# Three passes instead of two ahead of the memory rows' turn, later output passes, and a second work area for the left probabilities

## The chip, the core and the metric

The kernel runs on one core of a Trainium2 chip. The metric is the device time of one execution in microseconds (us). Before the change the median of three runs is 1904.54 us (1896.93 to 1905.54). Engines are named as in the profile: PE is the matrix engine (PEld its weight loads), DVE the vector engine, ACT the scalar engine, POOL and SP the two that issue most transfers. A transfer is a DMA.

## What is computed

The input is one sequence of 2048 rows of 1024 numbers, cut into 64 segments of 32 rows. Each segment is put behind 8 memory rows, goes through attention with 32 heads of 128, and its first 8 output rows are the memory of the next segment, so the segments form a chain.

```python
xn = layernorm(x)
for s in range(64):
    h = concat(mem, xn[32 * s:32 * s + 32])
    q, k, v = h @ Wq, h @ Wk, h @ Wv
    o = softmax(mask(q @ k.T * scale)) @ v @ Wo
    mem, out[s] = o[:8], o[8:]
return x + concat(out) + moe(xn)
```

The second summand, `moe`, picks two rows by a router score and sends them through a gated layer; it runs after the last segment.

## The kernel before

**Weights.** The three projections and the output projection are cut into 64 granules of 128 x 2048 (512 KB each). Granules 0 to 47 are six phases of eight (Wq, Wk for heads 0 to 15 and 16 to 31, then Wv), 48 to 63 are the output projection, two heads each. 44 granules are resident in on-chip memory. The 20 listed in `STREAMED` are loaded again for every segment, through five slots of a pool (`wstream`, tile `g`); two of them (6 whole, three quarters of 25) are kept in the PSUM memory and copied back, so 19 loads per segment are left. SP issues them in the order of use; a load waits until its slot has been read for the last time.

**Main rows and left rows.** A segment has 40 rows with the memory. 32 of them (8 memory rows and the first 24 rows of the segment) depend on the segment before and go through the phases as "main" rows (line L771, PSUM tile `PSm`, weights `ST`; output projection L571 into `WO`, weights `OT`). The last 8 rows of each segment, the "left" rows, depend on no memory for their q, k and v, so they are handled for four segments at once: a group `G` is four segments, `j` is the place of a segment in its group. For a group there are seven units of left passes: `q0`, `q1`, `k0`, `k1`, `v0`, `v1` with eight passes each (L564, tile `PSl`, weights `STL`), and `o`, the output projection, with 16 (L571 with tile `WL`, weights `OTL`). One pass is one granule times the left rows. All units share one PSUM tile (tag `accl`), so they run one after another.

**The order.** It is written out by hand. `PASSES` gives for each unit the places `(j, phase, kc)` and the granules whose passes run there; `kc` is the place in a phase of eight, phase 6 is the output projection (16 places), and 7 and 8 stand for the two places at the end of a segment. `COPIES` says where a finished unit is copied out of PSUM and on which engine. `hooks` do the same for attention work. Every engine runs its own queue in the order of this program.

**The end of a segment.** After the last output pass DVE adds the result to `X` (L840), PE turns the memory rows (L293, `mem_to_st`), DVE copies them into the next `ST` (L312), and the next segment's phase 0 begins. `run_passes(7, 0)` stands ahead of the turn, `run_passes(8, 0)` behind it:

```python
        nc.vector.tensor_tensor(out=OB[:, :], in0=WO[:, 0:256], in1=OB[:, :], op=ALU.add)
        ...
        run_passes(7, 0)
        if s + 1 < NSEG:
            mem_to_st(OB, nxt["st"])
        run_passes(8, 0)
```

**Attention of a segment.** `scores(half)`, `exponent()` (ACT, L663), `soften(half)` (DVE, L668 to L679) and `attend(half, ph)` (PE L693 and L695, then copies L702 into `OT` and L704 into `OTL`). `soften` writes the left probabilities into a zeroed work area, 8 blocks of 32 columns, and turns that with one 128x256 transpose (L679). For `j` of 1 to 3 the work area is the part of `OTL` that belongs to segment 3 of the group; at `j == 3` `attend(0, 0)` and `attend(0, 1)`, which stand behind `soften(1)` in the program, write the left outputs of heads 0 to 15 over the first half of it. At `j == 0` the work area is another tile, `BX`.

**The output rows of the left rows.** For unit `o` the sum with `x` is formed in tile `OL` (DVE, L593) and stored with four transfers of 16 KB by POOL (L596). `OL` has the tag `stl`, one buffer that it shares with `STL`, the turned left rows of the next group. `STL` is written by ACT (L307) in phase 6 at `w == 12` of the segment with `j == 0`, and the first user is the pass of unit `q0` at place (0, 7, 0). So at `j == 0` the four stores of `OL` must have landed before L307 may write.

Of the kernel before, what the change touches and what calls it, by code (L numbers as in the profile page):

```python
# [8 lines left out]
BF16 = mybir.dt.bfloat16  # L9
F32 = mybir.dt.float32  # L10
U32 = mybir.dt.uint32
ALU = mybir.AluOpType
# [17 lines left out]

UNIT_PHASE = {"q0": 0, "k0": 1, "q1": 2, "k1": 3, "v0": 4, "v1": 5, "o": 6}
PASSES = {
# [11 lines left out]
}  # L44

COPIES = {"q0": (1, 1, 0, "scalar"), "q1": (1, 5, 7, "vector"), "k0": (2, 2, 0, "scalar"), "k1": (3, 1, 0, "scalar"),
          "v0": (3, 4, 7, "scalar"), "v1": (3, 5, 7, "scalar"), "o": (0, 4, 3, "vector")}


@with_exitstack  # L50
def kernel(
# [16 lines left out]
    nc = tc.nc  # L68
    P = 128
# [3 lines left out]
    SEG = int(A_seg_len)  # L73
# [10 lines left out]
    XL = M  # L84
    NK = M + SEG
# [32 lines left out]
    one = ctx.enter_context(tc.tile_pool(name="one", bufs=1, reuse_waits="tile"))  # L118
# [78 lines left out]
    for s in range(4):  # L197
        nc.vector.tensor_copy(out=SELM[:, s, :, 0:XM],
                              in_=IDENT[:, 32 * s:32 * s + XM].unsqueeze(1).to_broadcast([P, 4, XM]))
        nc.vector.tensor_copy(out=SELL[:, s, :, :],  # L200
                              in_=IDENT.rearrange("p (s c) -> p s c", c=32)[:, :, XM:SEG])
# [304 lines left out]
    def left_out():  # L506
        if "otl" not in group:
            group["otl"] = one.tile([P, H, 4, XL], BF16, tag="otl", name="OTL")
        return group["otl"]
# [94 lines left out]
    for s in range(NSEG):  # L604
        G, j = divmod(s, 4)
# [6 lines left out]
        QT, KT, PTs, OT, nxt, sums = {}, {}, {}, {}, {}, {}  # L612
# [52 lines left out]
        def soften(half):  # L665
            S8 = SPS.rearrange("p i a k -> p (i a) k")
            DN = one.tile([P, 8], F32, tag="nm", name="DN")
            nc.vector.tensor_reduce(out=DN[:, :], in_=S8, axis=AX.X, op=ALU.add)  # L668
            nc.vector.reciprocal(out=DN[:, :], in_=DN[:, :])
            PT2 = one.tile([P, 2, 4, 64], BF16, tag=("bA", "bE")[half], name="PT2")  # L670
            PTm, PTl = PT2[:, 0], PT2[:, 1]
            PM = PTl.rearrange("p i q -> p (i q)").rearrange("p (b k) -> p b k", b=8)
            PLt = zeros_and_left()
            dnb = DN[:, :].unsqueeze(2)
            nc.vector.tensor_tensor(out=PM, in0=S8[:, :, 0:32], in1=dnb.to_broadcast([P, 8, 32]), op=ALU.mult)
            nc.vector.tensor_tensor(out=PLt[:, :, j, :], in0=S8[:, :, 32:NK],
                                    in1=dnb.to_broadcast([P, 8, XL]), op=ALU.mult)
            nc.vector.transpose(out=PTm.rearrange("p i q -> p (i q)"), in_=PM.rearrange("p b k -> p (b k)"))
            nc.vector.transpose(out=PTl.rearrange("p i q -> p (i q)"), in_=PLt.rearrange("p b s r -> p (b s) r"))  # L679
            PTs[half] = (PTm, PTl)  # L680

        def attend(half, ph, turn_too=None):
            if half not in OT:
                OT[half] = one.tile([P, 4, 4, SEG], BF16, tag=("kt", "bC")[half], name="OT")
                if half == 0:
                    nxt["wo"] = psA.tile([P, 512], F32, tag="acc", name="WO")
                sums[half] = [BS[:, 0:4 * NK] if half else nxt["wo"][:, 256:256 + 4 * NK], OPB]
            PTm, PTl = PTs[half]
            for il in range(4):
                for jl in range(2):  # L690
                    q0 = 32 * (2 * ph + jl)
                    o = sums[half][jl][:, il * NK:(il + 1) * NK]
                    nc.tensor.matmul(o, lhsT=VM[half][q0:q0 + 32, il * P:(il + 1) * P], rhs=PTm[q0:q0 + 32, il, 0:NK],  # L693
                                     start=True, stop=False, tile_position=(q0, 0), skip_group_check=True)
                    nc.tensor.matmul(o, lhsT=VL[half][q0:q0 + 32, il * P:(il + 1) * P], rhs=PTl[q0:q0 + 32, il, 0:NK],  # L695
                                     start=False, stop=True, tile_position=(q0, 0), skip_group_check=True)
            if turn_too is not None:
                turn_too()
            for jl in range(2):
                ov = sums[half][jl].rearrange("p (i q) -> p i q", i=4)  # L700
                copy = nc.scalar.copy if half == 0 or jl == 0 else nc.vector.tensor_copy
                copy(out=OT[half][:, 2 * ph + jl, :, :], in_=ov[:, :, 0:SEG])  # L702
                h0 = 16 * half + 8 * ph + 4 * jl
                copy(out=left_out()[:, h0:h0 + 4, j, :], in_=ov[:, :, SEG:NK])  # L704
# [3 lines left out]
        def zeros_and_left():  # L708

            z = left_out()[:, :, 3, :] if j or s == 0 else nxt["bx"][:, 0:256].rearrange("p (h r) -> p h r", r=XL)  # L710
            return z.rearrange("p (b s) r -> p b s r", s=4)
# [37 lines left out]
        hook(2, 6, lambda: scores(0))  # L749
        hook(3, 4, exponent)  # L750
        hook(3, 4, lambda: soften(0))
        if s + 1 < NSEG:
            hook(2, 4, lambda: load_seg(s + 1))
# [3 lines left out]
        hook(4, 6, lambda: scores(1))  # L757
        hook(5, 0, exponent)
        hook(5, 0, lambda: soften(1))
        hook(5, 4, lambda: attend(0, 0))  # L760
        hook(5, 6, lambda: attend(0, 1))

        for p, (mat, half) in enumerate(PHASES):
# [54 lines left out]
        for w in range(16):  # L818
            if w == 5:
                attend(1, 0)  # L820
            if w == 8 and s + 1 < NSEG:
                attend(1, 1, lambda: turned.append(turn(xn, BS[:, 160:288].bitcast(BF16))))
                nxt["st"] = new_st(turned[0])
            elif w == 8:
                attend(1, 1)
            if w == 12 and left_too is not None:
                STL = new_stl(turn(left_too))
            Gv = granule(48 + w)
            project(WO, w, Gv, lhs_main, w == 15, first=(w == 0))
            held[48 + w] = Gv  # L830
            run_passes(6, w)
            if w == 9 and s + 1 < NSEG:
                new_lx(s + 1)
                bring_back(1, nc.scalar.copy)
                bring_back(2, nc.vector.tensor_copy)
            if w == 11 and j == 3:
                xl_of[0] = load_left(G, one.tile([P, 256], BF16, tag="stl", name="OL")[:, :])
            release(6, w)
# [129 lines left out]
```

## Time and profile before

| what | value |
|---|---|
| median of 3 runs | 1904.54 us |
| the profiled execution, its own time | 1902.86 us |
| its span in the trace | 1901.0 us |
| granted TensorE clock, mean | 0.953 |
| PE busy | 1588.8 us (84%) |
| DVE busy | 895.1 us (47%) |
| ACT busy | 685.6 us (36%) |
| POOL busy | 441.7 us (23%) |
| bytes moved by DMA | 704.02 MB, mean 370 GB/s |
| the segments' adds (L840), first and last | 128.4 and 1843.0 us |

The span is the time from the first to the last instruction in the trace; the rest of the execution's own time lies around it. Busy matmul time is modelled and pipelined: four matmuls of 128x512 that belong to one pass follow each other at a few ns, and one row of the profile says 0.39 us for them, while passes follow each other every 0.21 us or so. A segment is the stretch between two rows of L840; in the middle of the run these lie some 27 us apart.

### The profile page before, as it was taken

To read this page: it belongs to the slowest core of one execution; us is meant where nothing else is said; L and a number is where in the kernel's file an instruction comes from. 1 tells how busy PE (TensorE), PEld (TensorE's weight loads), DVE (VectorE), ACT (ScalarE), POOL (GpSimd) and SP (SyncE) were. 2 spreads that over 40 slices of the span, in tenths; PEclk is the share of its full clock that TensorE was granted. 3 is DMA by queue.
4 is the path that set the end of the run, shared out by engine and by line. 5 is a ranking of instruction groups with operands and counts; after the bars stand their busy time and mean duration, and the time that the engine had idled before them with its cause. 6 is when DMAs were issued, how large, how long until landed. Compare 5 with 4: busy or idle time off the path is not lost.

```text
span 1901.0 us, 82443 instructions
## 1 busy us (share of the span) xinstructions
PE 1588.8 (84%) x36008; PEld 883.5 (46%) x36008; DVE 895.1 (47%) x2922; ACT 685.6 (36%) x1923; POOL 441.7 (23%) x882
## 2 busy tenths in 40 slices
PE   3658888888888898898888988988888888988864
PEld 1224545454454544445454544445454444545443
DVE  5824544455445544544455444544544454445430
ACT  1213333333343433343333333334333343433320
POOL 3211213222131222213121322213132221312220
PEclk8569999999999999999999999999999999999985
DMA  9999999999999999999999999999999999999998
GB/s 365 410 355 392 358 373 370 386 371 366 379 370 383 356 369 358 381 381 356 388 352 376 367 374 366 371 374 368 382 336 383 367 353 380 369 385 359 363 386 334
DMA packets 232089, 704.02 MB, mean 370 GB/s; under 512 B 39296, under 2 KB 61232, under 8 KB 231728
## 3 DMA queue, kind: packets, MB, share of 16 engines
q1 hardware_dynamic: 194384, 662.92, 91.9%
q0 software_dynamic: 28704, 27.96, 4.6%
q10 hardware_dynamic: 8640, 7.87, 1.2%
q8 instruction: 282, 4.62, 0.9%
q14 instruction: 79, 0.65, 0.1%
HBM read 685.93 MB, written 22.16 MB: 372 GB/s over the span
## 4 chain that ended last, share of the span: by engine, by line
DMA 54%; PE 37%; DVE 4%; issue 2%; ACT 1%; SPq 1%; ACTq 0%; DVEq 0%
DMA g<-wsc 45%; PE PSm L771 19%; PE WO L571 6%; PE PSl L564 3%; PE BT L621 3%; PE WL L571 2%; DMA XP<-in_A_x_dram 2%; DMA MW<-in_B_w_gate_dram 1%; DMA MW<-in_B_w_up_dram 1%; DMA g<-in_A_Wv_dram 1%; DMA g<-in_A_Wq_dram 1%; DMA wres<-in_A_Wv_dram 1%; DMA g<-in_A_Wk_dram 1%; DMA wres<-in_A_Wo_dram 1%; PE BS L644 1%
## 5 line engine op out<-in xcount | busy, mean ns | idle before, releaser
L771 PE MATMUL PSm<-wres,ST 128*32 128x512 bf16 x8448 | 710.6, 384 | 17.0 <-issue 8.6
L771 PEld LDWEIGHTS <-ST 128*32 128x32 bf16 x12288 | 329.1, 96 | 401.5 <-issue 186.8
L771 PE MATMUL PSm<-g,ST 128*32 128x512 bf16 x3588 | 363.4, 388 | 97.3 <-DMA g<-wsc 71.4
L571 PEld LDWEIGHTS <-OT 128*32 128x32 bf16 x8192 | 219.1, 98 | 152.0 <-issue 132.2
L790 ACT CAST XB<-PSm 128x512 bf16<-128x512 f32 x256 | 149.8, 585 | 312.8 <-PE PSm L771 308.1
L571 PE MATMUL WO<-wres,OT 128*32 128x256 bf16 x5632 | 242.7, 282 | 15.4 <-issue 8.4
L480 POOL DMA_DIRECT2D LX<-ql_d x63 | 33.6, 533 | 832.1 <-ACT OT L702 402.9
L571 PE MATMUL WO<-g,OT 128*32 128x256 bf16 x2560 | 134.3, 284 | 77.5 <-DMA g<-wsc 68.2
L564 PE MATMUL PSl<-wres,STL 128*32 128x512 bf16 x2112 | 191.9, 389 | 0.2 <-ACT VL L805 0.2
L842 POOL DMA_DIRECT2D out_dram<-X x256 | 129.5, 513 | 213.6 <-DVE X L840 165.5
L273 POOL DMA_DIRECT2D X<-in_A_x_dram x256 | 129.6, 511 | 187.1 <-PE PSm L771 88.1
L377 DVE COPY g<-BT 128x512 bf16<-128x512 bf16 x63 | 26.7, 425 | 307.2 <-ACT QT L629 256.5
L373 ACT COPY BK<-KEPT 128x512 bf16<-128x512 bf16 x126 | 75.8, 602 | 121.7 <-PE WO L571 121.7
L629 ACT COPY QT<-BT 128x512 bf16<-128x512 bf16 x128 | 74.9, 585 | 113.8 <-PE BT L621 113.1
L840 DVE TENSOR_TENSOR X<-WO,X 128x256 bf16<-128x256 f32 x64 | 27.2, 425 | 179.1 <-PE WO L571 179.1
L564 PEld LDWEIGHTS <-STL 128*32 128x32 bf16 x3072 | 83.9, 98 | 56.1 <-issue 9.8
L621 PEld LDWEIGHTS <-XB 128*128 128x128 bf16 x1024 | 58.9, 98 | 108.1 <-ACT XB L790 63.2
L693 PEld LDWEIGHTS <-VM 32*128 32x128 bf16 x2048 | 67.6, 91 | 85.1 <-issue 72.0
L800 ACT CAST VM<-PSm 128x512 bf16<-128x512 f32 x128 | 75.9, 593 | 78.1 <-PE PSm L771 76.7
L621 PE MATMUL BT<-IDENT,XB 128*128 128x128 bf16 x1024 | 102.6, 223 | 1.4 <-ACT QKL L499 1.4
L653 DVE TENSOR_TENSOR BS<-BS,CT 128x96 f32<-128x96 f32 (+1 forms) x256 | 59.6, 233 | 84.7 <-PE BS L646 80.2
L702 ACT CAST OT<-BS 128x128 bf16<-128x128 f32 x128 | 34.0, 265 | 181.3 <-PE BT L695 87.9
(170 smaller groups left out, 2428.2 us busy)
## 6 DMA issues: line engine op xcount, KB each, us to landing
g<-wsc SPq DMA_DIRECT2D x1134, 512.0 KB, 6.0
LX<-ql_d POOLq DMA_DIRECT2D x63, 128.0 KB, 5.9
g<-wsc SPq DMA_DIRECT2D x63, 128.0 KB, 5.2
ql_d<-XBl ACTq DMA_DIRECT2D x60, 128.0 KB, 5.4
MW<-in_B_w_gate_dram SPq DMA_DIRECT2D x16, 448.0 KB, 9.0
MW<-in_B_w_up_dram SPq DMA_DIRECT2D x16, 448.0 KB, 9.1
wres<-in_A_Wk_dram SPq DMA_DIRECT2D x12, 512.0 KB, 12.3
MW<-in_B_w_down_dram SPq DMA_DIRECT2D x12, 512.0 KB, 10.4
```

Of the source, the lines that this page charges most:

```text
L273: nc.gpsimd.dma_start(out=X[s % 2][32 * g:32 * g + XM, :], in_=x2[s * SEG:s * SEG + XM, 256 * g:256 * (g + 1)])
L373: copy(out=back[c][:, :], in_=KEPT_COLS[KEPT_WHOLE][c])
L564: nc.tensor.matmul(PSl[32 * jq:32 * jq + 32, :], lhsT=STL[:, g % KC, :], rhs=part(Gv, jq), start=first_, stop=last_, tile_position=(0, 32 ...
L571: nc.tensor.matmul(PS[32 * g:32 * g + 32, 0:256], lhsT=lhs(h), rhs=Gv[:, D * hs + 256 * g:D * hs + 256 * (g + 1)], start=(first and hs == ...
L621: nc.tensor.transpose(out=PTq[:, il, :, :].rearrange("p j r -> p (j r)"), in_=XB[:, il * P:(il + 1) * P], identity=IDENT[:, :])
L629: nc.scalar.copy(out=QT[half][:, :, :], in_=pv)
L653: nc.vector.tensor_tensor(out=S4, in0=S4, in1=m, op=ALU.add)
L693: nc.tensor.matmul(o, lhsT=VM[half][q0:q0 + 32, il * P:(il + 1) * P], rhs=PTm[q0:q0 + 32, il, 0:NK], start=True, stop=False, tile_position ...
L771: nc.tensor.matmul(PSm[32 * jq:32 * jq + 32, :], lhsT=ST[:, kc, :], rhs=part(Gv, jq), start=(kc == 0), stop=(kc == KC - 1), tile_position= ...
L790: nc.scalar.copy(out=XB[:, :], in_=PSm[:, :])
L800: nc.scalar.copy(out=VM[half][:, :], in_=PSm[:, :])
L842: nc.gpsimd.dma_start(out=out2[s * SEG:s * SEG + XM, 256 * g:256 * (g + 1)], in_=OB[32 * g:32 * g + XM, :])
```

## The change

Three edits, in one table and in two functions.

1. Units `q0`, `k0`, `k1` and `o` get three passes at place (j, 7, 0) and two at (j, 8, 0), where they had two and two. The fifth pass is taken from a place inside the phases: granule 7 from (1, 0, 7), 14 from (2, 1, 6), 24 from (2, 4, 1), 54 from (0, 0, 3). All the moved granules are resident.
2. The other output passes of the group before, at `j == 0`, start at (0, 2, 4) instead of (0, 0, 3) and end at (0, 5, 1) instead of (0, 4, 2); the sum and the stores of `OL` move from (0, 4, 3) to (0, 5, 3).
3. In `soften(1)` at `j == 3`, the work area is split. Blocks 0 to 3 are the new tile `Z`, 128 columns behind the 512 of `OT[0]` in the same buffer, zeroed by DVE; blocks 4 to 7 stay where they were. One product and one transpose become two of half the width. `attend` no longer makes `OT[0]` where `soften` has.

```diff
-    "q0": {(0, 7, 0): [0, 1], (0, 8, 0): [3, 4], (1, 0, 2): [2], (1, 0, 5): [5], (1, 0, 6): [6], (1, 0, 7): [7]},
+    "q0": {(0, 7, 0): [0, 1, 3], (0, 8, 0): [4, 7], (1, 0, 2): [2], (1, 0, 5): [5], (1, 0, 6): [6]},
...
-    "k0": {(1, 7, 0): [8, 10], (1, 8, 0): [11, 12], (2, 1, 1): [9], (2, 1, 5): [13], (2, 1, 6): [14], (2, 1, 7): [15]},
-    "k1": {(2, 3, 1): [25], (2, 3, 5): [29], (2, 4, 1): [24], (2, 4, 5): [26], (2, 7, 0): [27, 28], (2, 8, 0): [30, 31]},
+    "k0": {(1, 7, 0): [8, 10, 11], (1, 8, 0): [12, 14], (2, 1, 1): [9], (2, 1, 5): [13], (2, 1, 7): [15]},
+    "k1": {(2, 3, 1): [25], (2, 3, 5): [29], (2, 4, 5): [26], (2, 7, 0): [24, 27, 28], (2, 8, 0): [30, 31]},
...
-    "o": {(3, 6, 3): [50], (3, 6, 5): [53], (3, 6, 8): [56], (3, 6, 11): [59], (3, 6, 14): [62], (3, 7, 0): [48, 49],
-          (3, 8, 0): [51, 52], (0, 0, 3): [54], (0, 1, 1): [55], (0, 2, 0): [57], (0, 2, 4): [58], (0, 3, 0): [60],
-          (0, 3, 4): [61], (0, 4, 2): [63]},
+    "o": {(3, 6, 3): [50], (3, 6, 5): [53], (3, 6, 8): [56], (3, 6, 11): [59], (3, 6, 14): [62], (3, 7, 0): [48, 49, 51],
+          (3, 8, 0): [52, 54], (0, 2, 4): [55], (0, 3, 0): [57], (0, 3, 4): [58], (0, 4, 2): [60], (0, 4, 6): [61],
+          (0, 5, 1): [63]},
...
-          "v0": (3, 4, 7, "scalar"), "v1": (3, 5, 7, "scalar"), "o": (0, 4, 3, "vector")}
+          "v0": (3, 4, 7, "scalar"), "v1": (3, 5, 7, "scalar"), "o": (0, 5, 3, "vector")}
...
-            nc.vector.tensor_tensor(out=PLt[:, :, j, :], in0=S8[:, :, 32:NK],
-                                    in1=dnb.to_broadcast([P, 8, XL]), op=ALU.mult)
+            apart = half == 1 and j == 3
+            if apart:
+                OT[0] = one.tile([P, 640], BF16, tag="kt", name="OT")
+                Z = OT[0][:, 512:640]
+                nc.vector.memset(Z, 0.0)
+                parts = [(slice(0, 4), Z.rearrange("p (b s r) -> p b s r", b=4, s=4)), (slice(4, 8), PLt[:, 4:8])]
+                OT[0] = OT[0][:, 0:512].rearrange("p (i j r) -> p i j r", i=4, j=4)
+            else:
+                parts = [(slice(0, 8), PLt)]
+            for bs, z in parts:
+                n = bs.stop - bs.start
+                nc.vector.tensor_tensor(out=z[:, :, j, :], in0=S8[:, bs, 32:NK],
+                                        in1=dnb[:, bs].to_broadcast([P, n, XL]), op=ALU.mult)
             nc.vector.transpose(out=PTm.rearrange("p i q -> p (i q)"), in_=PM.rearrange("p b k -> p (b k)"))
-            nc.vector.transpose(out=PTl.rearrange("p i q -> p (i q)"), in_=PLt.rearrange("p b s r -> p (b s) r"))
+            for bs, z in parts:
+                nc.vector.transpose(out=PTl.rearrange("p i q -> p (i q)")[:, 32 * bs.start:32 * bs.stop],
+                                    in_=z.rearrange("p b s r -> p (b s) r"))
```

What it moves on the engines stands in the order of the program's instructions; a row names the line, the operation, and what is written from what, and where asked for, the semaphores that it waits for (`DVE_49` counts DVE's finished work, and so on).

On ACT, the copies behind `attend(0, 0)` in a segment with `j == 3`, before:

```order
L704 CAST OTL<-WO 128x4x8 [waits DVE_49,Pool_49]
L702 CAST OT<-BT 128x128 [waits PE_49]
L704 CAST OTL<-BT 128x4x8
L702 CAST OT<-WO 128x128 [waits PE_49]
L704 CAST OTL<-WO 128x4x8
```

and with the change (`attend` has moved down by 14 lines):

```order
L718 CAST OTL<-WO 128x4x8 [waits Pool_49]
L716 CAST OT<-BT 128x128 [waits PE_49]
L718 CAST OTL<-BT 128x4x8
L716 CAST OT<-WO 128x128 [waits PE_49]
L718 CAST OTL<-WO 128x4x8
```

The first copy into `OTL` no longer waits for DVE; its place and that of the others in ACT's queue are the same.

On PE, the matmuls at the end of a segment with `j == 0` (one row of each pass; `wres0` is resident granule 0, and so on), before:

```order
L571 MATMUL WO_24085<-wres63_1247,OT_24195 32x256
L564 MATMUL PSl_24351<-wres0_210,STL_24310 32x512
L564 MATMUL PSl_24351<-wres1_212,STL_24310 32x512
L293 MATMUL BT_134<-IDENT_125,X0_130 128x128
L564 MATMUL PSl_24351<-wres3_218,STL_24310 32x512
L564 MATMUL PSl_24351<-wres4_222,STL_24310 32x512
L771 MATMUL PSm_24371<-wres0_210,ST_24264 32x512
```

and with the change:

```order
L571 MATMUL WO_24109<-wres63_1247,OT_24219 32x256
L564 MATMUL PSl_24375<-wres0_210,STL_24334 32x512
L564 MATMUL PSl_24375<-wres1_212,STL_24334 32x512
L564 MATMUL PSl_24375<-wres3_218,STL_24334 32x512
L293 MATMUL BT_134<-IDENT_125,X0_130 128x128
L564 MATMUL PSl_24375<-wres4_222,STL_24334 32x512
L564 MATMUL PSl_24375<-wres7_228,STL_24334 32x512
L785 MATMUL PSm_24399<-wres0_210,ST_24288 32x512
```

One more pass stands ahead of the turn (L293), and granule 7's pass has come forward out of phase 0. The passes ahead of the turn read `STL`.

On DVE, the sum of the left output rows in a segment with `j == 0`, before (L679 ends `soften(0)`, the second L653 begins `scores(1)`):

```order
L679 STREAM_TRANSPOSE PT_23928<-BX 128x256 [waits DVE_49]
L593 TENSOR_TENSOR OL<-WL,OL 128x256 [waits PE_49]
L653 TENSOR_TENSOR BS<-BS,CT 128x4x24 [waits PE_49]
L655 TENSOR_SCALAR BS<-BS,CT 128x4x8 [waits DVE_49]
L653 TENSOR_TENSOR BS<-BS,CT 128x4x8 [waits DVE_49]
```

and with the change (L691 now ends `soften(1)`):

```order
L689 STREAM_TRANSPOSE PT_24068<-PT_24068 128x256 [waits DVE_49]
L691 STREAM_TRANSPOSE PT_24068<-BX 128x256 [waits DVE_49]
L593 TENSOR_TENSOR OL<-WL,OL 128x256 [waits PE_49]
L267 COPY RI<-BS 128x1
L268 RECIPROCAL RI<-BS 128x1
```

The sum has moved from between the two softmaxes of the segment to behind the second one, past the eleven rows from L653 to L679; POOL's four stores and, in ACT's queue, `STL` (L307) follow it as before.

More of the change, by code (lines that the diff above doesn't have):

```diff
@@ L675, in soften @@
             nc.vector.tensor_tensor(out=PM, in0=S8[:, :, 0:32], in1=dnb.to_broadcast([P, 8, 32]), op=ALU.mult)
-            nc.vector.tensor_tensor(out=PLt[:, :, j, :], in0=S8[:, :, 32:NK],
-                                    in1=dnb.to_broadcast([P, 8, XL]), op=ALU.mult)
+            apart = half == 1 and j == 3
[11 more added lines that the diff above has]
+                                        in1=dnb[:, bs].to_broadcast([P, n, XL]), op=ALU.mult)
             nc.vector.transpose(out=PTm.rearrange("p i q -> p (i q)"), in_=PM.rearrange("p b k -> p (b k)"))
-            nc.vector.transpose(out=PTl.rearrange("p i q -> p (i q)"), in_=PLt.rearrange("p b s r -> p (b s) r"))
+            for bs, z in parts:
+                nc.vector.transpose(out=PTl.rearrange("p i q -> p (i q)")[:, 32 * bs.start:32 * bs.stop],
+                                    in_=z.rearrange("p b s r -> p (b s) r"))
             PTs[half] = (PTm, PTl)
         def attend(half, ph, turn_too=None):
-            if half not in OT:
-                OT[half] = one.tile([P, 4, 4, SEG], BF16, tag=("kt", "bC")[half], name="OT")
+            if half not in sums:
+                if half not in OT:
+                    OT[half] = one.tile([P, 4, 4, SEG], BF16, tag=("kt", "bC")[half], name="OT")
                 if half == 0:
```

## The prediction

> **What bounds the kernel now.** I read the page's shares first, then the busy share of the transfers by stretches, then who waits for whom, then the timeline of one group of segments.
>
> ```profile
> PE 1588.8 (84%) x36008; PEld 883.5 (46%) x36008; DVE 895.1 (47%) x2922; ACT 685.6 (36%) x1923; POOL 441.7 (23%) x882
> q1 hardware_dynamic: 194384, 662.92, 91.9%
> DMA packets 232089, 704.02 MB, mean 370 GB/s; under 512 B 39296, under 2 KB 61232, under 8 KB 231728
> DMA 54%; PE 37%; DVE 4%; issue 2%; ACT 1%; SPq 1%; ACTq 0%; DVEq 0%
> ```
>
> The chain of waits changes between transfers (54%) and PE (37%): the streamed granules are the bound, and PE where it frees the slots late. q1 alone, SP's queue, takes 91.9% of the engines' time. So a microsecond of PE is worth something only where the transfers stand idle because of it. The stretches show where that is; the columns end with granted clock, DMA share and GB/s.
>
> ```profile
> 950.00:955.00 5.00, 5.00 (x120) 2.52 (x120) 3.53 (x11) 2.19 (x5) 0.00 (x0) 1.00 1.02 373
> 960.00:965.00 5.00, 4.14 (x138) 3.01 (x132) 2.31 (x10) 2.46 (x11) 0.00 (x0) 1.00 0.96 361
> 965.00:970.00 5.00, 3.06 (x107) 2.60 (x107) 0.72 (x3) 1.07 (x4) 2.88 (x5) 1.00 0.87 298
> 970.00:975.00 5.00, 4.49 (x101) 2.44 (x91) 0.95 (x3) 1.17 (x2) 3.52 (x7) 1.00 1.03 351
> 975.00:980.00 5.00, 4.33 (x78) 2.28 (x82) 1.74 (x7) 1.96 (x4) 3.20 (x6) 1.00 0.86 305
> 980.00:985.00 5.00, 5.00 (x128) 2.88 (x128) 4.04 (x14) 2.31 (x6) 0.00 (x0) 1.00 0.97 313
> 985.00:990.00 5.00, 4.36 (x122) 2.21 (x114) 3.76 (x12) 2.74 (x13) 2.40 (x4) 1.00 0.98 374
> 990.00:995.00 5.00, 3.55 (x122) 2.77 (x111) 3.22 (x16) 1.51 (x7) 0.37 (x1) 1.00 1.03 412
> 995.00:1000.00 5.00, 4.46 (x92) 2.11 (x84) 0.95 (x3) 1.33 (x3) 2.02 (x5) 1.00 1.03 392
> ```
>
> A full stretch shows 1.02 to 1.03. The segment with `j == 3` ends near 970 and that with `j == 0` near 997. From 960 to 990 the shares miss 0.07 + 0.16 + 0.00 + 0.17 + 0.06 + 0.05 = 0.51 of 5 us, so 2.5 us of transfer time are lost in this group, from the end of `j == 3` through most of `j == 0`. Behind that the transfers are full. All three edits touch this place, and 2.5 us is the most that they can win there.
>
> **The split work area.** The waits view and the timeline at that place:
>
> ```profile
> ACT OTL L704 <- DVE PT L679: 21.0, 16, 2.0
> PE WO L693 <- ACT OTL L704: 11.3, 19, 1.8
> ```
>
> ```profile
> 959.73 0.60 PE L564 MATMUL PSl<-wres,STL 128*32 128x512 bf16 x8
> 959.76 0.22 DVE L676 TENSOR_TENSOR OTL<-BS,DN 128x64 bf16<-128x64 f32 x1
> 960.36 0.45 DVE L679 STREAM_TRANSPOSE PT<-OTL 128x256 bf16<-128x256 bf16 x1
> 960.73 0.12 DVE L267 COPY RI<-BS 128x1 f32<-128x1 f32 x1
> 960.90 0.18 ACT L704 CAST OTL<-WO 128x32 bf16<-128x32 f32 x1 [1.46 <-DVE PT L679]
> 961.13 0.17 PE L693 MATMUL WO<-PT,VM 32*128 32x40 bf16 x1 [0.80 <-ACT OTL L704]
> 961.39 0.17 PE L693 MATMUL BT<-PT,VM 32*128 32x40 bf16 x1
> 962.13 0.35 DVE L284 TENSOR_SCALAR XN<-X,RI 128x256 bf16<-128x256 bf16 x1 [0.83 <-PE PSm L771]
> ```
>
> ACT may not write the left outputs over the work area before DVE has turned it (1.46 us idle here, 21.0 us in 16 segments), and PE's next `attend` waits for ACT's copy: 11.3 us, 0.7 us for each of 16 segments, and another 961.39 - 961.13 = 0.26 us until the second sum is free. With the split the first copies depend on PE alone, so PE wins about 0.95 us a group. DVE has three more rows, a memset and a second product and transpose, all of half the width. If the halves cost together what the whole did, only the memset is added, at least the 0.12 us of the small copy L267; if each half costs as much as the whole, it is 0.12 + 0.22 + 0.45 = 0.8 us. I take 0.5, since a half operation keeps some fixed part. It is covered by the 0.83 us in which DVE waits ahead of L284; with PE 0.95 us earlier that cover is gone, and then L284 is late by up to 0.5 us, but PE turns its result only at w == 8 of the output phase.
>
> **The third pass.** The end of the segment with `j == 0`:
>
> ```profile
> 997.00 0.40 PE L571 MATMUL WO<-wres,OT 128*32 128x256 bf16 x8
> 997.21 0.62 PE L564 MATMUL PSl<-wres,STL 128*32 128x512 bf16 x8
> 997.93 0.28 PE L293 MATMUL BT<-IDENT,X 128*128 128x128 bf16 x2
> 998.14 0.62 PE L564 MATMUL PSl<-wres,STL 128*32 128x512 bf16 x8
> 998.59 0.60 PE L771 MATMUL PSm<-wres,ST 128*32 128x512 bf16 x8
> ```
>
> Two passes start at 997.21 and take 2 x 0.22 us of issue (998.14 to 998.59 for two), so PE is free from 997.65 and waits for DVE's add until 997.93: 0.28 us, enough for a third pass. It is free, and 0.22 us less stand inside the phases. This counts in full at the end of `j == 3`. At the ends of `j == 1` and `j == 2` the transfers are nearly full (1.02 around 950); I give those two 0.06 us each, between nothing and 0.22.
>
> **Output passes late.** By phase 3 of `j == 0`, three output passes fewer than before stand ahead of PE (54 gone to the boundary, two shifted), up to 3 x 0.22 = 0.66 us earlier release of slots, which shrinks to 0.22 us or so by the end of phase 4. Together PE is 0.95 + 0.22 + up to 0.66 us earlier in the stretch that loses 2.5 us. Ends: nothing, when the loads then set the pace, and 1.8 us. Most of the idle time lies right behind the stall and right at the passes moved, so I take 1.1 us, and 16 x (1.1 + 0.12) = 20 us in all.
>
> **What it costs: STL waits.** The same move sends the sum of `OL` behind the second softmax, and `STL` shares its buffer.
>
> ```profile
> 985.18 0.38 DVE L593 TENSOR_TENSOR OL<-WL,OL 128x256 bf16<-128x256 f32 x1
> 990.16 0.45 DVE L679 STREAM_TRANSPOSE PT<-BX 128x256 bf16<-128x256 bf16 x1
> 985.86 2.40 POOL L596 DMA_DIRECT2D out_dram<-OL  x4 [6.87 <-DVE OL L593]
> 994.63 0.55 POOL L480 DMA_DIRECT2D LX<-ql_d  x1 [6.37 <-ACT OT L702]
> 996.21 0.37 ACT L307 COPY STL<-BT 128x256 bf16<-128x256 bf16 x1 [0.84 <-PE BT L293]
> 997.49 0.58 ACT L373 COPY BK<-KEPT 128x512 bf16<-128x512 bf16 x1 [0.91 <-PE WO L571]
> ```
>
> ```profile
> DMA to landing us min/median/max: 4.7/5.6/6.7
> ```
>
> Before, the last store is issued at 985.86 + 1.80 = 987.66 and lands at about 993.3, and L307 at 996.21 never sees it. After, the sum starts when the second softmax ends, about 990.55; the first store follows 0.68 us later as before, the last 1.80 us behind that, at 993.03. It lands at 997.7, 998.6 or 999.7 with the min, median and max of those stores. L307 takes 0.37 us and hands on in about 0.1, so the first q0 pass starts at 998.2, 999.1 or 1000.2 instead of 997.21: PE waits 1.0, 1.9 or 3.0 us; I take 1.9. Behind it in PE's queue stand the turn of the memory rows and the whole next segment. On ACT only L373 stands behind L307, and its copy is needed at kc = 6 of the next phase. On POOL the stores end at 993.6, before LX is issued at 994.63. The added 0.38 us on DVE lies ahead of L284 as well, with the output phase as cover. This happens in 14 groups (the first and the last have no such pair).
>
> How much of the 1.9 us the loads notice depends on how long a granule's load takes from issue to landing; a load that has queued has room. Three stretches, 965 to 975, 990 to 998 and 1003 to 1012:
>
> ```profile
> g<-wsc SPq DMA_DIRECT2D x5, 512.0 KB, 5.6
> ```
>
> ```profile
> g<-wsc SPq DMA_DIRECT2D x6, 512.0 KB, 7.2
> ```
>
> ```profile
> g<-wsc SPq DMA_DIRECT2D x7, 512.0 KB, 5.9
> ```
>
> Around the boundary a load spends 7.2 us, 1.6 more than in the stretch that ran dry (5.6 at share 0.87); but five to fifteen us later only 0.3 more. So of 1.9 us some 0.9 is absorbed (between 0.3 and 1.6, nearer to the middle) and 1.0 is lost: 14 us. Ends: 0.3 x 14 = 4 and 1.6 x 14 = 22 us.
>
> **Sum** against the profiled execution: 1902.86 - 20 + 14 = 1897 us. That execution lies 1.7 us under the median of the three runs, much less than what the terms leave open.
>
> **The rivals.** (1) The wait on STL is hidden. For it: the loads are 7.2 us deep there, and PE waits for granules later in that segment anyway, where it can catch up. Against: only 0.3 us of depth is left ten us on. Then the gain stands with 1 or 2 us of loss: 1902.86 - 20 + 1 = 1884. [...]
>
> (2) The wait is worse than the gain. The stores now run where the transfers are full (1.03 at 990 to 1000), not at 0.98 as before, and may land like the slowest, 6.7 us: PE waits 3.0 us, 0.9 is absorbed, 2.1 x 14 = 29 us are lost, and with a gain of 16 the time is 1902.86 - 16 + 29 = 1916. It decides from a wait of 20 / 14 + 0.9 = 2.3 us on, that is from a landing of 6.0 us.
>
> (3) The loads cannot go faster, PE's gains turn into waits for granules, and its late starts cost nothing either: 1903, no change. For it: 91.9% for q1. Against: 412 GB/s at 990 beside 298 at 965. [...]
>
> **How the numbers follow.** Forecast 0.43, with a range of its own of 1889 to 1906; rival 1 0.25, rival 2 0.20, rival 3 0.12. About 0.5%, 9.5 us, is what a measurement here can tell from no change: faster is below 1895, slower above 1914. The forecast's own range puts 0.17 below 1895, 0.24 between and 0.02 above. Faster: 0.25 + 0.17 = 0.42; same: 0.24 + 0.12 = 0.36; slower: 0.22. The range reaches to rivals 1 and 2, 1881 to 1916, leaving out the outer part of each. The time is the forecast's, 1897.
>
> **What would show it.** Right: no row of ACT's OTL waiting for DVE in the waits view; a new row of ACT's STL waiting for the stores, some 14 times and about 2 us each (L307 has been idle 0.84 us there); shares of 0.9 and more in the stretches that had 0.87 and 0.86; and lower shares in the first half of `j == 1`. Wrong: L307 still released by PE's turn (rival 1), a new wait of 2.5 us and more (rival 2), or PE's waits for granules up by as much as its waits for ACT went down (rival 3).

## The result, and the profile after

The change makes the kernel slower by 1.0%. The medians of five runs each are 1904.54 us (1896.93 to 1914.05) before and 1923.41 us (1919.61 to 1930.33) after; the ratio is 1.0102, with a 95% interval of 1.0062 to 1.0141. The predicted 1897 us and the range up to 1916 us are both missed, on the slow side. The profiled execution after has a span of 1921.7 us (before 1901.0), with a mean granted clock of 0.950 (0.953).

The page of the profile after, its lines on busy time, transfers and the chain that ended last:

```profile
PE 1593.2 (83%) x36008; PEld 879.7 (46%) x36008; DVE 897.7 (47%) x2970; ACT 682.5 (36%) x1923; POOL 441.6 (23%) x882
DMA packets 232090, 704.02 MB, mean 366 GB/s; under 512 B 39296, under 2 KB 61232, under 8 KB 231728
q1 hardware_dynamic: 194384, 662.92, 91.4%
DMA 57%; PE 39%; issue 2%; SPq 1%; DVE 0%; ACT 0%; ACTq 0%; DVEq 0%
DMA g<-wsc 44%; PE PSm L785 21%; PE PSl L564 6%; PE WO L571 4%; DMA out_dram<-OL 4%; PE BT L621 3%; PE WL L571 2%; DMA XP<-in_A_x_dram 2%; DMA MW<-in_B_w_gate_dram 1%; DMA g<-in_A_Wv_dram 1%; DMA MW<-in_B_w_up_dram 1%; DMA g<-in_A_Wq_dram 1%; DMA wres<-in_A_Wo_dram 1%; DMA g<-in_A_Wk_dram 1%; DMA wres<-in_A_Wv_dram 1%
```

The same bytes are moved, at 366 instead of 370 GB/s, so the transfers stand idle for longer. In the chain, DVE's 4% is gone, and 4% of the span now leads over the small stores of `OL`, four in a group, which were not in it before. The rows of the waits view for `STL` and for the granules before (engine, tile and line that waits, who ends it, sum in us, times, longest):

```profile
PE PSm L771 <- DMA g<-wsc: 71.4, 171, 2.1
PE WO L571 <- DMA g<-wsc: 68.2, 135, 1.9
ACT STL L307 <- PE BT L293: 17.5, 14, 6.9
```

and after:

```profile
ACT STL L307 <- DMA out_dram<-OL: 48.1, 14, 4.8
PEld L564 <- ACT STL L307: 27.4, 13, 3.4
PE PSl L564 <- ACT STL L307: 23.3, 13, 3.1
PE PSm L785 <- DMA g<-wsc: 74.9, 167, 1.7
PE WO L571 <- DMA g<-wsc: 62.0, 139, 1.4
```

The row of PE waiting for ACT's `OTL` (11.3 us before) is gone: the split does what it says. In its place stands ACT's `STL`, 14 times, behind the stores, and in 13 of these places PE's passes behind that: 23.3 / 13 = 1.8 us each. PE's waits for granules, 71.4 + 68.2 = 139.6 us before, are 136.9 us, nearly the same.

One such place, the end of segment 36 (`j == 0`), in the timeline (start, duration, engine and line, in brackets idle time and what ended it):

```profile
1112.97 0.45 DVE L691 STREAM_TRANSPOSE PT<-BX 128x256 bf16<-128x256 bf16 x1
1113.34 0.39 DVE L593 TENSOR_TENSOR OL<-WL,OL 128x256 bf16<-128x256 f32 x1
...
1114.02 2.40 POOL L596 DMA_DIRECT2D out_dram<-OL  x4 [11.76 <-DVE RI L268]
...
1121.84 0.37 ACT L307 COPY STL<-BT 128x256 bf16<-128x256 bf16 x1 [3.82 <-DMA out_dram<-OL]
...
1120.18 0.27 PE L571 MATMUL WO<-wres,OT 128*32 128x256 bf16 x1 [0.21 <-issue]
1122.27 0.92 PE L564 MATMUL PSl<-wres,STL 128*32 128x512 bf16 x12 [1.82 <-ACT STL L307]
1123.12 0.40 PE L293 MATMUL BT<-IDENT,X 128*128 128x128 bf16 x2
1123.44 1.04 PE L564 MATMUL PSl<-wres,STL 128*32 128x512 bf16 x8
1124.27 1.07 PE L785 MATMUL PSm<-wres,ST 128*32 128x512 bf16 x8
1125.12 0.64 PE L785 MATMUL PSm<-g,ST 128*32 128x512 bf16 x4
```

The chain is there link by link: the second softmax's last transpose, the sum right behind it, the stores, the copy, the passes. But look at the last rows: the eight matmuls of two passes that start at 1124.27 take until 1125.12, 0.85 us, where two passes took 0.45 us before (998.14 to 998.59). Behind its wait PE runs at half speed, at a granted clock of 0.50 from 1123 to 1125. The stretches show that, and what it does to the transfers; the last three columns are granted clock, DMA share and GB/s. After:

```profile
1119.00:1121.00 2.00, 1.07 (x24) 0.34 (x16) 0.42 (x1) 0.00 (x0) 0.00 (x0) 1.00 1.03 412
1121.00:1123.00 2.00, 0.73 (x12) 0.23 (x12) 0.00 (x0) 0.86 (x2) 1.80 (x4) 0.97 1.03 371
1123.00:1125.00 2.00, 2.00 (x22) 0.72 (x22) 0.52 (x2) 0.00 (x0) 0.56 (x2) 0.50 0.89 335
1125.00:1127.00 2.00, 2.00 (x28) 0.78 (x24) 0.00 (x0) 0.00 (x0) 0.00 (x0) 0.67 0.17 58
1127.00:1129.00 2.00, 2.00 (x39) 0.99 (x32) 0.00 (x0) 1.07 (x2) 1.67 (x4) 1.00 0.83 269
```

and the same place before (the segment ends at 1104.9):

```profile
1105.00:1107.00 2.00, 1.90 (x38) 0.80 (x34) 0.82 (x3) 0.50 (x1) 1.41 (x3) 1.00 1.03 365
1107.00:1109.00 2.00, 1.88 (x40) 0.92 (x32) 0.00 (x0) 0.03 (x1) 0.95 (x3) 1.00 1.00 396
1109.00:1111.00 2.00, 1.83 (x32) 0.82 (x24) 0.00 (x0) 1.31 (x3) 0.00 (x0) 1.00 1.04 383
```

While PE waits (1121) the transfers are still full, with a share of 1.03. They run dry, down to 0.17, some four to nine microseconds after the end of the segment, at 1120.5: PE started no pass over a streamed granule between 1119.48 and 1125.12, so no slot came free, and SP, which had issued a load at 1119.80, issued the next at 1126.24. Who looks only at the stretch of the wait sees nothing lost.

The lengths of the segments, from one of DVE's adds (L840, now L854) to the next, as means over 13 groups (segments 8 to 59) of each profiled execution, in us:

| kernel | j=0 | j=1 | j=2 | j=3 | group |
|---|---|---|---|---|---|
| before | 28.27 | 26.44 | 26.57 | 27.41 | 108.69 |
| after | 28.20 | 28.56 | 26.42 | 27.28 | 110.47 |
| stores ahead of the sum | 27.33 | 26.26 | 26.33 | 27.26 | 107.18 |
| split alone | 27.56 | 26.46 | 26.92 | 28.04 | 108.98 |
| third pass alone | 28.79 | 26.26 | 26.50 | 27.28 | 108.82 |
| late passes alone | 27.83 | 29.02 | 26.87 | 27.34 | 111.06 |
| sum early | 27.39 | 26.47 | 26.38 | 27.95 | 108.19 |
| split and third pass | 28.09 | 26.69 | 26.42 | 27.16 | 108.36 |
| PE kept busy | 27.19 | 28.09 | 26.62 | 27.47 | 109.37 |
| the same, tiny products | 27.69 | 28.84 | 26.37 | 27.42 | 110.32 |

The loss is in `j == 1` alone, right behind the wait: 28.56 - 26.44 = 2.1 us for each of 14 groups, 30 us. Single segments of one kind scatter by 0.4 to 2.4 us (one standard deviation), so a mean of 13 is good to 0.1 to 0.7 us, and smaller differences are not read.

### The profile page after: what moved, and what is told of

It is laid out like the page before. It is cut to its first block, busy times and chain, and to the rows that moved or that the text cites. A ratio compares the mean times of both kernels' runs of the same rounds, so it can differ in the third digit from the quotient of the medians.

```text
span 1921.7 us, 82489 instructions
## 1 busy us (share of the span) xinstructions
PE 1593.2 (83%) x36008; PEld 879.7 (46%) x36008; DVE 897.7 (47%) x2970; ACT 682.5 (36%) x1923; POOL 441.6 (23%) x882
## 3 DMA queue, kind: packets, MB, share of 16 engines
q8 instruction: 282, 4.62, 0.9%
## 4 chain that ended last, share of the span: by engine, by line
DMA 57%; PE 39%; issue 2%; SPq 1%; DVE 0%; ACT 0%; ACTq 0%; DVEq 0%
DMA g<-wsc 44%; PE PSm L785 21%; PE PSl L564 6%; PE WO L571 4%; DMA out_dram<-OL 4%; PE BT L621 3%; PE WL L571 2%; DMA XP<-in_A_x_dram 2%; DMA MW<-in_B_w_gate_dram 1%; DMA g<-in_A_Wv_dram 1%; DMA MW<-in_B_w_up_dram 1%; DMA g<-in_A_Wq_dram 1%; DMA wres<-in_A_Wo_dram 1%; DMA g<-in_A_Wk_dram 1%; DMA wres<-in_A_Wv_dram 1%
## 5 line engine op out<-in xcount | busy, mean ns | idle before, releaser
L571 PE MATMUL WO<-wres,OT 128*32 128x256 bf16 x5632 | 238.7, 277 | 19.5 <-issue 12.1
L564 PE MATMUL PSl<-wres,STL 128*32 128x512 bf16 x2112 | 191.8, 404 | 24.0 <-ACT STL L307 23.3
L854 DVE TENSOR_TENSOR X<-WO,X 128x256 bf16<-128x256 f32 x64 | 27.2, 424 | 188.0 <-PE WO L571 188.0
L653 DVE TENSOR_TENSOR BS<-BS,CT 128x96 f32<-128x96 f32 (+1 forms) x256 | 59.5, 232 | 92.9 <-PE BS L646 88.4
L668 DVE TENSOR_REDUCE DN<-BS 128x8 f32<-128x320 f32 x128 | 62.9, 492 | 71.9 <-ACT BS L663 71.9
## 6 DMA issues: line engine op xcount, KB each, us to landing
MW<-in_B_w_down_dram SPq DMA_DIRECT2D x12, 512.0 KB, 10.2
```

The costliest lines, as they stand in the source:

```text
L564: nc.tensor.matmul(PSl[32 * jq:32 * jq + 32, :], lhsT=STL[:, g % KC, :], rhs=part(Gv, jq), start=first_, stop=last_, tile_position=(0, 32 ...
L571: nc.tensor.matmul(PS[32 * g:32 * g + 32, 0:256], lhsT=lhs(h), rhs=Gv[:, D * hs + 256 * g:D * hs + 256 * (g + 1)], start=(first and hs == ...
```

## The experiments

Each ratio is to the kernel before, timed again beside that run (medians of 1905 to 1909 us).

**Stores ahead of the sum.** Theory A: the loss is the wait of `STL` for the stores. Theory B: it comes from something else in the change. The four stores (`store_left` holds the three lines taken out) move ahead of the sum:

```diff
-            o4 = out2[4 * Gu * SEG:4 * (Gu + 1) * SEG, :].rearrange("(s r) d -> s r d", s=4)
-            for g in range(4):
-                nc.gpsimd.dma_start(out=o4[:, XM:SEG, 256 * g:256 * (g + 1)], in_=OL[32 * g:32 * (g + 1), :])
+            if s + 1 == NSEG:
+                store_left(OL, Gu)
...
+            hook(2, 5, lambda: store_left(xl_of[0], G - 1))
```

> The changed kernel, but the four stores of the left rows go out at (0, 2, 5), ahead of the sum with the output projection, so the left rows of all groups but the last leave without their projection; the sum itself still runs at (0, 5, 3), and bytes and rows are the same. Theory A (the late stores hold STL, and nearly the whole loss is that wait and what follows it): the 14 waits of ACT's L307 for the stores vanish, the segments with j = 1 go back from 28.6 to about 26.5 us, and the time falls by 25 to 35 us, to 1890 to 1898. Rival B (the new order of passes starves the loads by itself, and the wait only takes the place of waits for granules): the waits vanish, and the time stays within 8 us of the changed kernel, 1915 and above.

Measured: ratio 0.9920 (0.9886 to 0.9953), 1893.5 us. In its waits view `STL` waits for PE's turn alone, as before the change:

```profile
ACT STL L307 <- PE BT L293: 17.1, 13, 6.9
```

The segment with `j == 1` is 26.26 us long. Theory A holds: without that wait the same passes at the same places make the kernel faster by 0.8%.

**The three parts alone.** Each is put into the kernel before by itself. The split is the diff's part in `soften` and `attend`. The third pass, at the ends of all four segments of a group:

```diff
-    "q0": {(0, 7, 0): [0, 1], (0, 8, 0): [3, 4], (1, 0, 2): [2], (1, 0, 5): [5], (1, 0, 6): [6], (1, 0, 7): [7]},
+    "q0": {(0, 7, 0): [0, 1, 3], (0, 8, 0): [4, 7], (1, 0, 2): [2], (1, 0, 5): [5], (1, 0, 6): [6]},
```

(`k0`, `k1` and `o` likewise). The late passes, with the sum:

```diff
-          (3, 8, 0): [51, 52], (0, 0, 3): [54], (0, 1, 1): [55], (0, 2, 0): [57], (0, 2, 4): [58], (0, 3, 0): [60],
-          (0, 3, 4): [61], (0, 4, 2): [63]},
+          (3, 8, 0): [51, 52], (0, 2, 0): [54], (0, 2, 4): [55], (0, 3, 0): [57], (0, 3, 4): [58], (0, 4, 2): [60], (0, 4, 6): [61],
+          (0, 5, 1): [63]},
...
-          "v0": (3, 4, 7, "scalar"), "v1": (3, 5, 7, "scalar"), "o": (0, 4, 3, "vector")}
+          "v0": (3, 4, 7, "scalar"), "v1": (3, 5, 7, "scalar"), "o": (0, 5, 3, "vector")}
```

> The kernel before with only the split work area. Prediction on record: PE wins 0.95 us in each of 16 groups and most of it reaches the time, ratio to before 0.992. Theory C (PE's waits that no row of the profile ends, at every 256th instruction of its queue, grow by what the split wins): PE's 11.3 us of waits for OTL go to about 0, the unexplained waits in the same stretch grow by some 8 to 15 us, ratio 0.996 to 1.000. Rival: the three added rows of DVE cost time, ratio above 1.002.

> The kernel before with only the third pass ahead of the turn (q0, k0, k1, o), the other output passes and the sum of the left rows where they were. Theory A: a small gain or nothing, ratio 0.995 to 1.000; no wait of L307 for stores. Rival B (the order of passes itself is bad): 1.003 and above.

> The kernel before with only the late output passes and the late sum and stores (granule 54's pass at (0, 2, 0), the rest as in the change; two and two passes at the segments' ends, no split). Theory A: the whole loss is here, ratio 1.010 to 1.018, 14 waits of L307 for the stores of about 2 us at PE. Rival B: the loss is shared with the third pass, ratio 1.002 to 1.008.

Measured: the split 0.9965 (0.9939 to 0.9990), the third pass 0.9980 (0.9951 to 1.0010), the late passes 1.0109 (1.0062 to 1.0156). The three multiply to 1.0054, 0.5% under the whole change, which their intervals allow. The late passes carry the whole loss; their waits view has the row of the changed kernel:

```profile
ACT STL L307 <- DMA out_dram<-OL: 52.8, 14, 4.8
PE PSl L564 <- ACT STL L307: 24.5, 14, 3.0
```

The split alone wins 0.35% (6.7 us) and the third pass something between 0.5% won and 0.1% lost. The split's view shows where some of its gain went:

```profile
PE WO L571 <- issue: 19.8, 16, 3.0
PE WO L707 <- ACT OTL L718: 0.9, 3, 0.6
```

The first of these rows before:

```profile
PE WO L571 <- issue: 8.7, 13, 1.9
```

The 11.3 us of waits for `OTL` are 0.9, but PE's waits that no row ends ("issue"), ahead of output passes, are 19.8 us instead of 8.7. The last section comes back to them.

**The sum early.** Granule 63's pass and the copy of the unit move a few places forward, and with them the sum ahead of the second softmax:

```diff
-          (0, 5, 1): [63]},
+          (0, 5, 0): [63]},
...
-          "v0": (3, 4, 7, "scalar"), "v1": (3, 5, 7, "scalar"), "o": (0, 5, 3, "vector")}
+          "v0": (3, 4, 7, "scalar"), "v1": (3, 5, 7, "scalar"), "o": (0, 5, 0, "vector")}
```

> The changed kernel, but granule 63's pass and the copy of the output unit move from phase 5, places 1 and 3, to place 0, so that the sum of OL stands ahead of the second softmax of j = 0 on DVE, and its four stores start some 4 us earlier. Theory A (the loss is the wait of STL for those stores): the row of L307 waiting for the stores falls from 48 us to under 8 us, the segment with j = 1 goes back from 28.6 to about 26.4 us, and the time is as in the run with the stores ahead of the sum, 0.990 to 0.996 of the kernel before (about 1895 us). Theory B (the loss comes from the late passes themselves, which keep PE from reading granules in phase 5): two of the passes now stand even closer together, the segment with j = 1 stays above 28 us and the ratio is 1.005 or more.

Measured: 0.9945 (0.9918 to 0.9972), 1894.52 us; `j == 1` 26.47 us. Its waits view, and `STL` in its timeline at the end of segment 36:

```profile
ACT STL L307 <- PE BT L293: 23.2, 15, 7.0
```

```profile
1106.13 0.37 ACT L307 COPY STL<-BT 128x256 bf16<-128x256 bf16 x1 [0.33 <-PE BT L293]
```

Theory A holds again, B falls. This is the whole change but for one pass and the sum a few places earlier, and it is faster than both kernels: 0.55% under the kernel before, and 1.0102 - 0.9945 = 1.57% or 30 us under the changed one (20 to 39 us with both intervals), as much as the 14 x 2.1 us read from the segments.

**Split and third pass, the other passes and the sum as before.** Against the changed kernel:

```diff
-          (3, 8, 0): [52, 54], (0, 2, 4): [55], (0, 3, 0): [57], (0, 3, 4): [58], (0, 4, 2): [60], (0, 4, 6): [61],
-          (0, 5, 1): [63]},
+          (3, 8, 0): [52, 54], (0, 1, 1): [55], (0, 2, 0): [57], (0, 2, 4): [58], (0, 3, 0): [60],
+          (0, 3, 4): [61], (0, 4, 2): [63]},
...
-          "v0": (3, 4, 7, "scalar"), "v1": (3, 5, 7, "scalar"), "o": (0, 5, 3, "vector")}
+          "v0": (3, 4, 7, "scalar"), "v1": (3, 5, 7, "scalar"), "o": (0, 4, 3, "vector")}
```

> The kernel before with the split work area and the third pass at three of the four ends of segments; the output passes left over keep early places, and the sum of OL stands where it stood. Theory A: no wait of STL, and the gains of the two parts alone (0.9965 and 0.998) add: 0.993 to 0.997, about 1896 us. If the late passes bring a gain of their own, as the prediction has it, this run is slower than the one with the sum early by 0.2% or more; if the two agree within 0.2%, the late passes bring nothing that can be measured.

The third pass stands at all four ends here, not at three as the expectation says. Measured: 0.9979 (0.9958 to 1.0001), just past the end of what theory A gave, so the two gains do not add up in full. It is slower than the run with the sum early by 0.34%, as the prediction's third term would have it; the two intervals overlap, so that the late passes win something is likely and not settled.

**PE kept busy in the wait.** 14 products that nobody reads, between the end of `j == 0` and the waiting passes:

```diff
+        if j == 0 and 0 < G < NT - 1:
+            for _ in range(14):
+                nc.tensor.matmul(BS[:, 0:256], lhsT=IDENT[:, :], rhs=res_tiles[0][:, 0:256], start=True, stop=True,
+                                 skip_group_check=True)
```

> The changed kernel with 14 added products of 128x256, from a resident granule into a part of PSUM that nothing reads then, at the end of each segment with j = 0, ahead of the passes that wait for STL: PE is busy some 1.5 us of the 1.9 us in which it waits. Theory C (the clock that fell to half rate behind the wait is a part of the loss, some 0.7 us of 2.1 us a group): stretches at half rate behind that end of a segment fall from 9 to 3 or fewer, the segment with j = 1 is 0.5 us shorter or more, and the time about 10 us under the changed kernel's (ratio near 1.005). Rival: the half rate is a mark of the wait, and the loads set the pace behind it anyway: the stretches vanish, the segment with j = 1 stays at 28.5 us, ratio 1.010 or more.

And the control, with `0:2` for `0:256`:

> A control for the run with 14 added products of 128x256: the same 14 products at the same place, but 2 columns wide, so PE has the same instructions and is busy for 14 x 27 ns = 0.4 us instead of some 1.5 us. Theory C (the half rate behind the wait costs what that run won): the stretches at half rate behind the end of j = 0 come back (5 or more), the segment with j = 1 is 28.4 us or more, ratio near 1.010. Rival (that run won by where its 28 more instructions put the stalls in which PE waits for its own instructions): segments, stalls and ratio as in that run, 28.1 us and 1.005.

Measured: 1.0050 (1.0032 to 1.0069) with the wide products, 1.0077 (1.0043 to 1.0112) with the tiny ones. In the record of the granted clock the changed kernel has 7 stretches at 0.5 just behind the end of a segment with `j == 0` (of 15, 58.0 us in all, between segments 4 and 61; the expectation's count of 9 was too high), the kernel before none there (of 10, 37.5 us), the wide products none (of 8) and the tiny ones 9 (of 14; two of the 9 begin some 2 us ahead of the end and reach over it). The stretches last 3.413 or 6.827 us. The same place in both, the end of segment 36, wide:

```profile
1117.45 1.70 PE L859 MATMUL BS<-wres,IDENT 128*128 128x256 bf16 x14
1119.09 0.83 PE L564 MATMUL PSl<-wres,STL 128*32 128x512 bf16 x12
...
1120.51 0.60 PE L785 MATMUL PSm<-wres,ST 128*32 128x512 bf16 x8
1120.94 0.39 PE L785 MATMUL PSm<-g,ST 128*32 128x512 bf16 x4
```

```profile
1119.00:1121.00 2.00, 2.00 (x36) 0.76 (x38) 0.52 (x2) 0.50 (x2) 1.65 (x4) 1.00 1.02 342
1121.00:1123.00 2.00, 2.00 (x44) 1.01 (x40) 0.00 (x0) 0.00 (x0) 0.00 (x0) 1.00 1.02 369
```

and tiny:

```profile
1117.71 1.47 PE L564 MATMUL PSl<-wres,STL 128*32 128x512 bf16 x12 [1.48 <-ACT STL L307]
...
1120.26 1.07 PE L785 MATMUL PSm<-wres,ST 128*32 128x512 bf16 x8
1121.12 0.64 PE L785 MATMUL PSm<-g,ST 128*32 128x512 bf16 x4
```

```profile
1119.00:1121.00 2.00, 2.00 (x22) 0.72 (x22) 0.52 (x2) 0.00 (x0) 0.00 (x0) 0.50 0.84 331
1121.00:1123.00 2.00, 2.00 (x24) 0.79 (x20) 0.00 (x0) 0.00 (x0) 0.00 (x0) 0.50 0.10 31
```

The eight matmuls of two passes take 1120.94 - 1120.51 = 0.43 us in the one and 1121.12 - 1120.26 = 0.86 us in the other, and the transfers, full in the one, fall to a share of 0.10 in the other. From the last output pass of `j == 0` to the first streamed granule of `j == 1` PE takes, as a mean over 13 groups, 1.89 us before and 4.53 us after; of the 2.64 us more, 1.88 are the wait itself and 0.76 nearly all the half rate (with the stores ahead of the sum, where the order is the same and nothing waits, it is 0.05 more than before). With the wide products it is 4.16 us with a wait (products included) that is 2.22 longer than before: 2.27 in all, so 0.05 are left and none of it is the clock's. With the tiny ones a wait of 1.69 grows to 2.53, 0.84 behind it.

The means of `j == 1` lie as theory C has them, 0.5 us shorter with the wide products than in the changed kernel and 0.75 us shorter than in the control. But these differences are hardly larger than what the means are good to, the intervals of the timed ratios overlap, and the wide run's `j == 0` is a microsecond shorter too, which theory C does not explain. The segments with `j == 1`, sorted by whether the granted clock fell to 0.5 in them, say more (number of segments; mean time from the last output pass to the first waiting pass; mean length, in us):

| kernel | clock full | clock at half for a time |
|---|---|---|
| after | 6; 1.29; 26.82 | 7; 2.53; 30.06 |
| late passes alone | 6; 1.51; 27.07 | 7; 2.47; 30.69 |
| PE kept busy | 13; 2.30; 28.09 | none |
| the same, tiny products | 4; 1.76; 27.84 | 9; 1.77; 29.29 |

In the control both kinds waited equally long, and those with the half rate are 29.29 - 27.84 = 1.45 us longer (standard error 0.4). The transfers agree: from 4 to 8 us behind the end of `j == 0` their mean share is 1.01 before, 0.65 after, 0.83 with the wide products and 0.68 with the tiny ones. So theory C holds, though the control's timed ratio lies half way between what the two theories gave. What the clock costs is an estimate: 7 x 1.45 = 10 us from the control, 14 x 0.5 to 14 x 0.75, 7 to 10 us, from the means.

**Where PE's unexplained stalls stand.** 64 small products are added at the very start, in the kernel before and in the one with the sum early:

```diff
+    for _ in range(64):
+        nc.tensor.matmul(OPB[:, 0:2], lhsT=IDENT[:, 0:128], rhs=IDENT[:, 0:2], start=True, stop=True, skip_group_check=True)
```

> The kernel before with 128 more PE instructions at its start (64 small products into a part of PSUM not used yet), nothing else. Theory D (PE's stalls that no row ends come from fetching its instructions, in pieces of 256): they stand at the same numbers in PE's order, 193 modulo 256, so at other places of the program than before; the time is within 0.4% of the kernel before. Rival (they belong to a place in the program, such as the first passes of a segment): they stay at the same lines and segments, at numbers moved by 128.

> The kernel with the sum ahead of the second softmax, with 64 small products (128 PE instructions) added at its start. Theory D: PE's stalls that no row ends stand again at numbers 193 modulo 256, at other places of the program; if their places decide 0.3% or more of the time, this run differs from the one without the products by as much, else both are within 0.3% of each other, near 0.9945 of the kernel before.

Measured: 0.9988 (0.9963 to 1.0014) and 0.9959 (0.9931 to 0.9987), both within 0.3% of the kernels without the products. Stalls of PE of 0.8 us and more that no row ends, in segments 8 to 59: 20 before the change, 16 with the shift, 23 in the changed kernel, 23 with the sum early, 20 with the sum early and the shift. Counted in PE's own order of instructions (weight loads, matmuls and the 228 records of its sequencer), every one of these 102 ends at a number that is 193 modulo 256. So theory D holds in its numbers: the stalls follow the count, not the place in the program, and where they fall is worth less than the timed runs can tell.

## Why the prediction was wrong

**What bounds the kernel** was read rightly: the transfers, and PE where it frees slots late (57% and 39% of the chain after, 54% and 37% before). The loss came in exactly that way, and the gain without the wait too.

**The mechanism of the loss** was named, with its place, its number (14 groups) and its link: a new row of `STL` behind the stores, and lower shares in the first half of `j == 1`. The wait was sized at 1.9 us from stores of 4.7, 5.6 and 6.7 us to landing and the sum's new place. It measured 1.88 us as a mean, single ones from 0 to 3.3; the view of the stores' line after has

```profile
DMA to landing us min/median/max: 4.6/5.6/6.7
```

**The step that failed** is the price of that wait: "So of 1.9 us some 0.9 is absorbed (between 0.3 and 1.6, nearer to the middle) and 1.0 is lost: 14 us." The runs show 2.1 us lost a group, 30 us. The sum had no term for the clock; it counts PE at full rate behind the wait. Where the rate stayed full, its step was near: in the 29 such segments of the table above a wait of 1.78 us (over the kernel before) lengthens the segment by 27.58 - 26.44 = 1.14 us, so some 0.6 us is absorbed, inside the bounds given. But in 7 of the 13 profiled groups of the changed kernel PE ran at half rate for 3.4 us or 6.8 us behind the wait, and those segments are 30.06 - 26.44 = 3.6 us longer, the other six 0.4 us. The first streamed granule is then not 1.9 us late but 2.64 as a mean, and the half rate goes on behind it. By the control's 1.45 us the clock is some 10 of the 30 us. The other 20 us, 1.4 us a group, stand against the 14 that were priced; that difference of 0.4 us a group is no larger than the scatter of the means.

**The gain of 20 us** was too large, by the medians by a quarter to a half: 0.8% or 15 us with the stores ahead of the sum (9 to 22 by its interval), 0.55% or 10.5 us with the sum early (5 to 16). In the changed kernel itself the profiled segments other than `j == 1` are only 0.35 us a group shorter, but those of the kernels that share its `j == 0` scatter from 27.2 to 28.2 us, so one execution does not size it. The sign that the prediction asked for is there: the mean share of the transfers in the two stretches of 4 us ahead of the end of `j == 3` is 0.92 and 0.87 before, 0.97 and 0.96 after, which is 0.56 us a group or 9 us in 16; 0.36 us of that is lost again 4 to 12 us behind that end. A part that can be named is the stalls at the end of `j == 3`: 4.1 us in segments 8 to 59 before, 10.2 us after, 14.6 us with the sum early. PE reaches the end of that segment sooner and stalls there instead. That they would be covered if PE still waited for `OTL` is argued from the sums, not tried.

**Rivals.** Rival 1 (a hidden wait, 1884 us) fell: the stores land where the traces of before had them, after 5.6 us in the median and 4.6 at the least (5.6 and 4.7 before). Rival 2 came nearest, 1916 us, and by sign it is what happened; but it asked for landings of 6.0 us and a wait of 2.3 us and more, and the median stayed at 5.6 us. That its loss of 2.1 us a group is the measured one is chance: it came from a shorter wait, with the clock. Rival 3 (loads that cannot go faster) fell with the two runs without the wait, at 0.992 and 0.9945.

## What to carry to other kernels

Where a pool of load slots feeds the engine, a wait of that engine is to be priced at the loads that are issued late because of it: in the place shown the transfers were full during the wait (a share of 1.03) and fell to 0.17 in the 4 to 9 us behind the end of the segment. Before work is moved late, list what shares its buffers: here one pass and one sum a few places earlier turned 1.0% slower into 0.55% faster with nothing else changed. A wait of some 2 us on the matrix engine cost more than its length here where the granted clock fell to 0.5 behind it: in the control, at equal waits of 1.8 us, 1.45 us more than where the clock stayed full.

## What was not expected of the hardware

**The clock fell behind a wait of 1.9 us.** In 7 of 14 such places of the changed kernel the granted clock was 0.5 for 3.413 or 6.827 us, beginning between 0.6 and 3.2 us into the next segment, and with 1.7 us of products in the same place in none. In each of the twelve profiles, all stretches at 0.5 between segments 4 and 61 begin on one grid of 3.413 us, to within 3 ns. By the modelled times of its matmuls, PE was idle for more than half of 90 steps of these grids, and 67 of them were followed by a stretch at 0.5, among them every one that was idle for 0.58 and more; of some 5200 steps idle for less than 0.38, 13 were. In the place shown PE waited for 1.82 us, and the step ahead of the stretch at 0.5, 3.413 us long, was idle for 0.59. What sets the clock is not shown beyond these counts.

**PE stalls at 193 modulo 256 in its count of instructions.** The 102 stalls that end at 193 modulo 256 take 0.8 to 3.1 us each, from the start of PE's instruction ahead to that of the next. The profile of the changed kernel has a queue for instructions:

```profile
q8 instruction: 282, 4.62, 0.9%
```

282 packets of together 4.62 MB are 16.4 KB each, and PE's 36008 matmuls, 36008 weight loads and 228 records of its sequencer are 72244 / 256 = 282 pieces of 256 instructions. Each stall ends 1.0 to 1.7 us after such a packet has landed. That PE waits there for its instructions is the author's reading of these three agreements and of the shift above; no row of the profile names what ends the stalls. The timeline shows one stall, in front of number 44737 of PE's order, in both kernels, behind the 11th matmul of a row of left output passes. Before:

```profile
1185.88 0.50 PE L571 MATMUL WL<-wres,OTL 128*32 128x256 bf16 x11
1187.99 0.38 PE L571 MATMUL WL<-wres,OTL 128*32 128x256 bf16 x5 [1.61 <-issue]
```

After:

```profile
1201.54 0.51 PE L571 MATMUL WL<-wres,OTL 128*32 128x256 bf16 x11
1204.14 0.60 PE L571 MATMUL WL<-wres,OTL 128*32 128x256 bf16 x13 [2.10 <-issue]
```

Most of them stand at the end of `j == 3` and in `j == 0`; why there was not tried. In segments 8 to 59 such stalls take 29.7 us together before the change and 39.4 us after.
